# The third batch's first quad takes its memory weights through a turn in DRAM in place of five TensorE transposes, with two instruction orders drawn up again

## The chip, the cores and the metric

One NeuronCore of a Trainium2 chip runs the whole program. The metric is the device time of one execution in microseconds (us), the median of several runs.

## The reference, cut to what matters

Eight batches, eight heads, 576 rows (`S`), head width 64, 32 memory slots (`M`); `d_model` is 512.

```python
a = softmax(phi, over the 576 rows)           # phi: batch, head, 576, 32
k_m = einsum('bhsm,bhsd->bhmd', a, k)         # keys and values of the 32 slots
v_m = einsum('bhsm,bhsd->bhmd', a, v)
attn = softmax(q @ k_m.T / 8)                 # 576 x 32 for each head
x = attn @ v_m                                # heads side by side: 576 x 512
u = x + (relu(x.T @ w_tok1) @ w_tok2).T       # mixing over rows, 256 wide
out = u + relu(u @ w_ch1) @ w_ch2             # mixing over channels, 1536 wide
```

## The kernel before

**Quads.** Four heads of a batch form a quad; there are sixteen, named here (batch, half). A quad's 4 x 32 slots fill the 128 partitions. For each quad the kernel takes the softmax of phi over rows (`phi_max` on DVE, `phi_exp` on ACT, `scales`/`phi_scale` on DVE), multiplies the weights with keys and values (`get_kv`, L641 or `mm_kv`, L1482: 20 matmuls into `kvp`), spreads the keys (`spread_T`), turns them (`turn_T`), copies them (`get_kb`), and forms the scores (`scores`, tiles `sp`). Their softmax goes out to DRAM and back by rows (`rows_out` L517, `rows_in` L524), is split in a high and a low part (`nat`), and the token mixing follows: `A` (tile `Ap`), `R` (`Rp`), and four products `u`, whose results are split in `uh` (ACT, L198) and `ul` (DVE, L201).

**Chunks.** The rows of all batches are cut in nine chunks of 512 columns. Chunks 0 to 2 go through the channel mixing directly: `mm_1` (L144, tile `cp`, 12 matmuls for each of 12 blocks), a relu split in `hh` and `hl`, and `ch2` (L167, tile `acc`). Chunks 3 to 8 go in three pairs through another scheme (`Pair`, `Run`, L298 and L2318), which fills the second half of the program.

**Three ways to the weights of phi.** `kvp` needs the exponentials with rows on the partitions. The quads of batches 0 and 1 (`EarlyQuad`) load phi so that the softmax runs along the free axis and then turn it by five TensorE transposes of 128x128 (`phi_turn`, L1125, tiles `pp`), which ACT copies out of PSUM (`phi_get`, L1148). The quads from (2,1) on (`LateQuad`) load another layout (`in_phi_turned_dram`, tile `phiT`), turn blocks of 32x32 on DVE (`phi_turn`, L628), write the result to DRAM (`phi_out`, two DMAs of L517, tensor `turns`) and read it back rearranged (`phi_in`, two DMAs of L524). Quad (2,0), here `second`, is of its own class `ThirdBatchQuad` and goes the first way, by transposes.

**Two orders.** The instruction order is written out, not found at run time. `step` registers a piece of work with its engine, its cost in us, what it waits for, and the rooms (buffers, PSUM banks) that it takes or uses; `plan` runs through them with a rank for each step and gives every engine its order; the steps are then issued in that order. It is done twice. The first order (numbers `RANKS`, L1043) covers the weights' conversion (`piece`), quads (0,0) to (1,1), chunk 0, and for (2,0) the loads and its turning of phi. The second (numbers `PLACES`, L2110) covers the other quads, from `get_kv` of (2,0) on, and chunks 1 and 2. The steps' costs stand beside them: `scores` 1.0 us, `get_kv` 1.25 us. In the first order `ps_tile` puts in matmuls of the identity with itself (L1075, `z.fill` of them) where the plan leaves TensorE a gap ahead of a step that takes a bank.

Each engine works through its own queue in order, SP's queue of DMA issues too. TensorE writes PSUM banks of three kinds (`at`, two; `acc0` to `acc3`; `ch`, two). The transposes of (2,0) take two `at` banks; its `kvp` takes a `ch` bank.

```python
            s.x_t = z = step(
                "PE", 0.65, lambda: s.phi_turn([b0, b1]), z, take=[b0, b1], use=[s.phi]
            )
...
    second = ThirdBatchQuad(2, 0)
    second.phi, kv2, q2 = Room(("phi", 2)), Room(("kv", 1)), Room(("qT", 1))
    second.l_phi = step("SP", 0.5, second.load_phi, take=[second.phi], move=0.9)
    z = second.plan_phi()
```

Of the kernel before, what the change touches and what calls it, by code (L numbers as in the profile page):

```python
# [10 lines left out]
F32 = mybir.dt.float32  # L11
# [9 lines left out]
P = 128  # L21
# [7 lines left out]
def kernel(  # L29
# [936 lines left out]
    def plan(rank, ways, slack=0.0, margin=0.85, behind=1e9):  # L966
# [644 lines left out]
    class ThirdBatchQuad(SecondQuad):  # L1611

        for name in (
            "turn_T", "get_kb", "scores", "S_take", "turn_S", "rows_in", "nat_low", "a_high", "a_low",
            "v_pair", "A", "R", "u", "straight", "u_high", "u_low", "spill", "store_u",
        ):
            locals()[name] = vars(LateQuad)[name]

        def spread_v(s, room):
            LateQuad.vb_room(s, room)  # L1620
            s.spread_values(s.vb, s.kvp[:, D : 2 * D])

        def get_kv(s):
            s.kvp = pch.tile([P, CW], F32, tag="ch", name="kvp" + s.n, bufs=2)
            s.mm_kv()

# [135 lines left out]
    second = ThirdBatchQuad(2, 0)  # L1762
    second.phi, kv2, q2 = Room(("phi", 2)), Room(("kv", 1)), Room(("qT", 1))
    second.l_phi = step("SP", 0.5, second.load_phi, take=[second.phi], move=0.9)
    z = second.plan_phi()
# [3 lines left out]
    for x in range(NKK):  # L1769
# [5 lines left out]
        "END", 0, None, z, second.scaled, took2, products[-1], *ready[NF - 1][:2],  # L1775
        *(y for Q in range(2) for y in quads[1, Q].lows + quads[1, Q].highs),
        use=[*PartC2.held, *room1, rest_room, second.phi, second.ptr, second.colr, kv2, q2, o0, *accs, *ready[NF - 1][2:], *room0],
# [15 lines left out]
    ahead = [(quads[1, 0].x_u[3].end, late[1].load_turned)] + [(118.0, late[1].phi_max)]  # L1793
# [11 lines left out]
    def room(tag, n=1):  # L1805
        return Room((tag, n))
# [7 lines left out]
    kv2, q2, pt2 = room("kv"), room("qT"), room("aT")  # L1814
# [3 lines left out]
        take=[*sum(c1_rooms, []), *u_rooms[1], o_rooms[0], rest_room, *hidden[0, NF - 1], kv2, q2, pt2, turned1, col1],  # L1818
# [46 lines left out]
    for n, qd in enumerate(late):  # L1865
        t0, do = later(n)
        if not n:
            qd.kvuse, qd.after, qd.q_r, qd.lq = [pt2, kv2], [begin], q2, begin
            continue
# [7 lines left out]
        z = do(-38, "ACT", 0.8, qd.phi_exp, y, use=[turned, col])  # L1877
# [10 lines left out]
    got_kv = do(-9, "PE", 1.25, second.get_kv, begin, take=[bank_rooms[0]], use=second.kvuse)  # L1888
    for n, qd in enumerate(late):
        t0, do = later(n)  # L1890
        bk, kb, vh, vl, vb = bank_rooms[n], kb_rooms[n], vh_rooms[n], vl_rooms[n], Room(("side vb", 1), ("vb", 1))
        T = room("kb") if n else room("pr", 2)
        z = got_kv
        if n:
            y = do(-8, "ACT", 0.37, qd.spread_T, z, qd.scaled, take=[T], use=[bk, qd.colr])
        else:
            y = do(-8, "DVE", 0.35, qd.spread_T, z, take=[T], use=[bk])
        v = do(-8, "DVE", 0.48, lambda qd=qd, r=vb: qd.spread_v(r), z, qd.scaled if n else y, sided, take=[vb], use=[bk, side_room] + [qd.colr] * (n > 0))
# [8 lines left out]
        z = do(0, "PE", 1.0, qd.scores, y, qd.lq, take=[*ss, S_], use=[qd.q_r, kb])  # L1907
        if nx:
            got_kv = do(0.1, "PE", 1.25, nx.get_kv, z, *nx.after, *vlows[-1:], take=[bank_rooms[n + 1]], use=nx.kvuse)
# [196 lines left out]
    for n in range(AHEAD):  # L2106
# [424 lines left out]
```

## Time and profile before

| what | value |
|---|---|
| median of 3 runs (lowest, highest) | 716.09 us (715.88, 717.05) |
| the profiled execution's own time | 718.54 us |
| its span, first to last instruction | 716.8 us |
| TensorE busy | 706.3 us, 99% |
| VectorE (DVE), ScalarE (ACT), GpSimd (POOL) busy | 521.9, 372.2, 60.2 us |
| bytes moved by DMA, mean rate | 157.08 MB, 219 GB/s |

The profiled execution is 2.45 us above the median; 1.74 us of it lie outside the span. In the rows further down `PEld` is TensorE's weight load, which runs beside its matmuls; a start is counted from the span's first instruction; what stands in square brackets is the idle time ahead of a row and what ended it. An f32 matmul is recorded as two, so a step of 20 shows as x40.

### The profile page before, as it was taken

How to read it: one execution, taken by the hardware profiler on the slowest of the kernel's cores; microseconds unless marked ns; L12 is line 12 of the kernel's file. 1: busy time of each engine (PE TensorE's matmuls, PEld its weight loads, DVE VectorE, ACT ScalarE, POOL GpSimd, SP SyncE). 2: the span in 40 equal slices, each digit the busy share in tenths (PEclk: the TensorE clock that was granted, in tenths of full speed). 3: DMA queues.
4: the chain of work that ended last, by engine and by line, in shares of the span. 5: the costliest groups of instructions: out<-in, count | busy, mean ns of one | idle time of the engine just before them, and what ended most of it. 6: DMA issues, size and time to landing. Idle time of an engine off the chain costs nothing.

```text
span 716.8 us, 11389 instructions
## 1 busy us (share of the span) xinstructions
PE 706.3 (99%) x4305; PEld 587.8 (82%) x4305; DVE 521.9 (73%) x861; ACT 372.2 (52%) x697; POOL 60.2 (8%) x64
## 2 busy tenths in 40 slices
PE   8899999999999999999999999999999999999998
PEld 8678888778888788889888888888888888788887
DVE  5999973877878986788665669976238976426983
ACT  6899774335455266546554465425346444436450
POOL 2133114010012201011100000000000000000000
PEclk9999999999999999999999999999999999999999
DMA  9966440878979999836627875284658074658202
GB/s 357 415 252 253 122 154 18 309 252 283 302 272 300 325 374 320 273 113 212 214 90 268 293 273 197 85 282 132 206 196 303 31 262 149 201 181 292 91 29 89
DMA packets 75334, 157.08 MB, mean 219 GB/s; under 512 B 16144, under 2 KB 38416, under 8 KB 70928
## 3 DMA queue, kind: packets, MB, share of 16 engines
q1 hardware_dynamic: 61600, 102.29, 40.4%
q10 hardware_dynamic: 13680, 54.07, 23.0%
q8 instruction: 34, 0.56, 0.3%
q14 instruction: 20, 0.16, 0.1%
HBM read 115.93 MB, written 40.40 MB: 218 GB/s over the span
## 4 chain that ended last, share of the span: by engine, by line
PE 86%; DMA 7%; DVE 5%; issue 1%; ACT 1%; SPq 0%; DVEq 0%; ACTq 0%
PE ma L298 13%; PE acc L167 12%; PE cp L144 12%; PE mU L2318 10%; PE mB L2318 7%; PE mc L298 7%; PE u L748 6%; PE mD L2318 3%; PE mA L2318 3%; PE mb L298 3%; PE Ap L551 3%; DMA phiT<-in_phi_turned_dram 2%; DMA raww<-in_w_tok_dram 2%; PE kvp L641 1%; DMA unit<-sums 1%; PE u L567 1%
## 5 line engine op out<-in xcount | busy, mean ns | idle before, releaser
L167 PE MATMUL acc<-hh,c 128*128 128x512 f32 x288 | 101.5, 399 | 0.0
L167 PEld LDWEIGHTS acc<-hh,c 128*128 128x128 f32 x288 | 54.1, 188 | 13.6 <-issue 2.6
L167 PE MATMUL acc<-hl,c 128*128 128x512 f32 x144 | 56.3, 391 | 0.0
L144 PE MATMUL cp<-uh,c1h 128*128 128x512 f32 x144 | 52.0, 402 | 0.4 <-DVE col L623 0.4
L144 PE MATMUL cp<-ul,c1h 128*128 128x512 f32 x144 | 50.5, 391 | 0.0
L144 PE MATMUL cp<-uh,c1l 128*128 128x512 f32 x144 | 50.4, 390 | 0.0
L2304 ACT CAST rT<-hid 128x512 fp32r<-128x512 f32 x54 | 32.1, 623 | 26.7 <-PE mB L2318 15.6
L2305 DVE TENSOR_TENSOR rT<-hid,rT 128x512 fp32r<-128x512 f32 x54 | 35.8, 686 | 6.7 <-ACT rT L2304 6.7
L691 POOL TENSOR_TENSOR nat<-side,nat 128x512 fp32r<-128x512 f32 (+1 forms) x24 | 22.8, 951 | 179.9 <-ACT nat L682 134.6
L2172 DVE TENSOR_TENSOR hid<-mb,hid 128x512 f32<-128x512 f32 x12 | 8.3, 692 | 39.0 <-ACT hid L2252 37.8
L114 ACT ACTIVATE hh<-cp 128x512 fp32r<-128x512 f32 x36 | 21.6, 599 | 24.4 <-PE cp L144 22.0
L117 DVE SCALAR_TENSOR_TENSOR hl<-cp,hh 128x512 fp32r<-128x512 f32 x36 | 24.6, 683 | 12.9 <-ACT hh L114 12.7
L144 PEld LDWEIGHTS cp<-uh,c1h 128*128 128x128 f32 x144 | 26.7, 188 | 8.7 <-issue 3.4
L2175 ACT ACTIVATE hid<-hid 128x512 f32<-128x512 f32 x24 | 15.2, 634 | 34.7 <-DVE hid L2172 34.7
L758 ACT COPY side<-u 128x288 f32<-128x288 f32 (+1 forms) x44 | 17.1, 392 | 28.9 <-PE u L748 26.8
L144 PEld LDWEIGHTS cp<-uh,c1l 128*128 128x128 f32 x144 | 27.0, 188 | 5.9
L144 PEld LDWEIGHTS cp<-ul,c1h 128*128 128x128 f32 x144 | 27.1, 188 | 4.6
L2304 ACT CAST r<-hid 128x512 fp32r<-128x512 f32 x36 | 22.5, 625 | 15.8 <-PE mU L2318 5.3
L167 PEld LDWEIGHTS acc<-hl,c 128*128 128x128 f32 x144 | 27.1, 188 | 4.1
L2305 DVE TENSOR_TENSOR r<-hid,r 128x512 fp32r<-128x512 f32 x36 | 24.7, 687 | 5.4 <-ACT r L2304 5.4
L298 PE MATMUL ma<-xrest_p,unit 128*128 128x512 f32 x108 | 27.4, 389 | 0.0
L748 PE MATMUL u<-w2h,Rh 128*128 128x288 f32 x96 | 27.0, 296 | 0.0
(380 smaller groups left out, 1900.9 us busy)
## 6 DMA issues: line engine op xcount, KB each, us to landing
unit<-sums ACTq DMA_DIRECT2D x54, 512.0 KB, 5.0
kv<-in_kv_dram ACTq DMA_DIRECT2D x11, 1280.0 KB, 8.3
rawc<-in_w_ch_dram SPq DMA_DIRECT2D x12, 1024.0 KB, 9.1
q<-in_q_dram ACTq DMA_DIRECT2D x11, 576.0 KB, 5.4
sums<-sums SPq DMA_DIRECT2D x12, 512.0 KB, 5.5
u_p<-spilled SPq DMA_DIRECT2D x6, 1024.0 KB, 6.6
unit<-sums ACTq DMA_DIRECT2D x18, 256.0 KB, 3.9
out_dram<-u_p SPq DMA_DIRECT2D x9, 512.0 KB, 2.8
```

Source lines behind the costliest of these rows:

```text
L114: nc.scalar.activation(out=h, in_=ps, func=AF.Relu)
L117: nc.vector.scalar_tensor_tensor(out=l, in0=ps, scalar=0.0, in1=f32(h), op0=ALU.max, op1=ALU.subtract)
L144: nc.tensor.matmul(ps, l[:, a], r[:, a], start=n == 0, stop=n == len(mm) - 1)
L167: nc.tensor.matmul(ps, l_[f // 2][:, f % 2, a * P : (a + 1) * P], r[:, w], start=f == start and x == 0, stop=f == end - 1 and x == 2,)
L298: nc.tensor.matmul(ps, l, r, start=first and n == 0, stop=n == len(mm) - 1, skip_group_check=not first,)
L551: nc.tensor.matmul(ps[:, :TT], a, w, start=x == 0, stop=x == len(mm) - 1)
L691: eng.tensor_tensor(out=o, in0=a, in1=f32(h), op=ALU.subtract)
L748: nc.tensor.matmul(s.up[db, hf][:, :HALF], a, r, start=x == 0, stop=x == len(mm) - 1)
L758: nc.scalar.copy(out=side[0][:, o + n : o + HALF], in_=ps[:, n:HALF])
L2304: nc.scalar.copy(out=t[:, 0], in_=x)
L2305: nc.vector.tensor_tensor(out=t[:, 1], in0=x, in1=f32(t[:, 0]), op=ALU.subtract)
L2318: nc.tensor.matmul(s.banks[room][a][:, w], l_[:, a * P : a * P + P], r_, start=not (p or x) and name in ("11", "T1", "21", "T4"), stop=p = ...
```

## The change

Quad (2,0) becomes a `LateQuad`. Its phi is loaded turned, its blocks are turned on DVE, written to DRAM and read back rearranged, within the first order; the five transposes, their two ACT copies and the class `ThirdBatchQuad` go. Its keys are spread on ACT in place of DVE. In the second order the cost of `scores` is 0.65 us (1.0 before), that of `get_kv` 1.36 us (1.25), that of `phi_exp` 0.88 us (0.8). Both tables of numbers are new, and with them the place of every step.

```diff
     RANKS = (
-        782, 764, 736, 674, 772, 710, 644, 470, 574, 316, 176, 288, 108, 64, 136, 122, 774, 216, 54,
+        784, 754, 704, 660, 774, 692, 568, 280, 448, 688, 182, 524, 160, 416, 86, 246, 778, 358,
...
-    class ThirdBatchQuad(SecondQuad):
...
-    second = ThirdBatchQuad(2, 0)
-    second.phi, kv2, q2 = Room(("phi", 2)), Room(("kv", 1)), Room(("qT", 1))
-    second.l_phi = step("SP", 0.5, second.load_phi, take=[second.phi], move=0.9)
-    z = second.plan_phi()
+    second = LateQuad(2, 0)
+    turned2, col2, phi2, kv2, q2 = (Room(x) for x in (("al", 2), ("ps", 2), ("phi", 2), ("kv", 1), ("qT", 1)))
+    z = step("SP", 0.5, second.load_turned, take=[turned2], move=0.81)
+    z = step("DVE", 0.78, second.phi_max, z, take=[col2], use=[turned2])
+    z = step("ACT", 1.0, second.phi_exp, z, use=[turned2, col2])
+    scaled = step("DVE", 0.38, second.scales, z, use=[col2])
+    turn2 = z = step("DVE", 0.8, second.phi_turn, z, take=[phi2], use=[turned2])
+    z = step("SP", 0.9, second.phi_out, z, use=[phi2], move=0.81)
+    z.lands = True
+    z = step("SP", 0.9, second.phi_in, z, use=[phi2], move=1.18)
...
-    ahead = [(quads[1, 0].x_u[3].end, late[1].load_turned)] + [(118.0, late[1].phi_max)]
+    ahead = [(turn2.end, late[1].load_turned), (max(turn2.end + 4.0, 118.0), late[1].phi_max)]
...
-        z = do(-38, "ACT", 0.8, qd.phi_exp, y, use=[turned, col])
+        z = do(-38, "ACT", 0.88, qd.phi_exp, y, use=[turned, col])
...
-    got_kv = do(-9, "PE", 1.25, second.get_kv, begin, take=[bank_rooms[0]], use=second.kvuse)
+    got_kv = do(-9, "PE", 1.36, second.get_kv, begin, take=[bank_rooms[0]], use=second.kvuse)
...
-        T = room("kb") if n else room("pr", 2)
+        T = room("kb")
         z = got_kv
-        if n:
-            y = do(-8, "ACT", 0.37, qd.spread_T, z, qd.scaled, take=[T], use=[bk, qd.colr])
-        else:
-            y = do(-8, "DVE", 0.35, qd.spread_T, z, take=[T], use=[bk])
...
+        y = do(-8, "ACT", 0.37, qd.spread_T, z, qd.scaled, take=[T], use=[bk, qd.colr])
...
-        z = do(0, "PE", 1.0, qd.scores, y, qd.lq, take=[*ss, S_], use=[qd.q_r, kb])
+        z = do(0, "PE", 0.65, qd.scores, y, qd.lq, take=[*ss, S_], use=[qd.q_r, kb])
...
-    order = plan(dict(zip(steps, PLACES, strict=True)), dict.fromkeys(steps, 0), 0.3969, 3.3, 5.0043)
+    order = plan(dict(zip(steps, PLACES, strict=True)), dict.fromkeys(steps, 0), 0.3837, 3.1511, 4.9562)
```

The diff leaves one thing unsaid that the counts of the orders show: over the program TensorE issues 5 transposes fewer and 9 identity matmuls more; DVE gets the turn of (2,0), one pass of a magnitude from ACT, and the low parts of a weight piece and of an attention operand from POOL, and gives one spreading of keys to ACT.

**TensorE at the end of the first order**, where quad (1,1) ends (`u11_1_1`), (2,0) begins and chunk 1 follows. Before:

```order
L567 MATMUL u11_1_1_1348<-w2l_97,Rh_1_1_1289 128x288
L567 MATMUL u11_1_1_1348<-w2h_96,Rl_1_1_1291 128x288
L1125 MATMUL pp0_2_0_1362<-ident_74,phi_2_0_163 128x128 x4
L1125 MATMUL pp1_2_0_1363<-ident_74,phi_2_0_163 128x128
L1482 MATMUL kvp_2_0_1379<-kv_2_0_799,pt_2_0_1369 32x128 x20
L144 MATMUL cp0_1_1409<-uh_1_864,c1h0_486 128x512
```

And now:

```order
L567 MATMUL u11_1_1_1365<-w2l_97,Rh_1_1_1287 128x288
L567 MATMUL u11_1_1_1365<-w2h_96,Rl_1_1_1290 128x288
L641 MATMUL kvp_2_0_1386<-kv_2_0_756,phi_2_0_561 32x128 x20
L144 MATMUL cp0_1_1415<-uh_1_847,c1h0_512 128x512
L144 MATMUL cp0_1_1415<-ul_1_848,c1h0_512 128x512
```

The two rows of transposes are gone, and the keys and values follow the last `u`.

**SP's queue in the first 20 us** (`raww2` is w_tok2, `rawc1_0` the first blocks of w_ch1, `rawc1_4` later ones). Before:

```order
L1093 DMA q_0_1_127<-in_q_dram 128x1152
L876 DMA raww2_1_131<-in_w_tok2_dram 128x1152
L876 DMA raww2_0_134<-in_w_tok2_dram 128x1152
L1255 DMA v_0_1_136<-in_kv_dram 128x1280
L896 DMA rawc1_0_158<-in_w_ch1_dram 128x2048
L896 DMA rawc1_4_160<-in_w_ch1_dram 128x2048
L1097 DMA phi_2_0_163<-in_phi_dram 128x640
L922 DMA rawc2_0_167<-in_w_ch2_dram 128x2048
L1097 DMA phi_1_0_219<-in_phi_dram 128x640
```

And now:

```order
L610 DMA phiT_2_0_127<-in_phi_turned_dram 128x576
L1093 DMA q_0_1_131<-in_q_dram 128x1152
L876 DMA raww2_1_134<-in_w_tok2_dram 128x1152
L876 DMA raww2_0_136<-in_w_tok2_dram 128x1152
L1255 DMA v_0_1_158<-in_kv_dram 128x1280
L896 DMA rawc1_4_160<-in_w_ch1_dram 128x2048
L1097 DMA phi_1_0_163<-in_phi_dram 128x640
L896 DMA rawc1_0_167<-in_w_ch1_dram 128x2048
L922 DMA rawc2_0_172<-in_w_ch2_dram 128x2048
```

The turned phi of (2,0) stands ahead of q, both pieces of w_tok2 and v; the first piece of w_ch1 has moved behind `rawc1_4` and the phi of (1,0).

**TensorE where chunk 0 begins** (`Tp` is the keys' transpose of (1,0), `cp0_0` the first product of chunk 0). Before:

```order
L1482 MATMUL kvp_1_0_556<-kv_1_0_299,pt_1_0_549 32x128 x20
L144 MATMUL cp0_0_586<-uh_0_474,c1h0_486 128x512 x4
L144 MATMUL cp0_0_586<-ul_0_475,c1h0_486 128x512 x4
L144 MATMUL cp0_0_586<-uh_0_474,c1l0_487 128x512 x4
L1500 MATMUL Tp_1_0_607<-ident_74,T_1_0_582 128x128
L144 MATMUL cp1_0_609<-uh_0_474,c1h0_486 128x512 x4
```

And now:

```order
L1482 MATMUL kvp_1_0_565<-kv_1_0_302,pt_1_0_540 32x128 x20
L1075 MATMUL Tp_1_0_603<-ident_74 128x128 x2
L1500 MATMUL Tp_1_0_603<-ident_74,T_1_0_597 128x128
L1075 MATMUL sp0_1_0_618<-ident_74 128x128 x2
L463 MATMUL sp0_1_0_618<-q_1_0_269,kb_1_0_612 32x288
L463 MATMUL sp1_1_0_621<-q_1_0_269,kb_1_0_612 32x288
```

Before, the first product of chunk 0 stood between the keys and values of (1,0) and their transpose, and the scores came after the second product; now transpose and scores (six more rows of `sp`) come ahead of the first product, with two identity matmuls in front of each.

## Rows read from the trace of the kernel before

**Rows 1.** The page's first part: busy time, share of the span, instructions.
```profile
PE 706.3 (99%) x4305; PEld 587.8 (82%) x4305; DVE 521.9 (73%) x861; ACT 372.2 (52%) x697; POOL 60.2 (8%) x64
```
**Rows 2.** Stretches: length, busy of each engine (x instructions), PEclk, DMA share, GB/s.
```profile
0.00:41.86 41.86, 37.34 (x416) 31.73 (x416) 31.78 (x58) 32.63 (x59) 9.39 (x22) 1.00 0.96 385
41.86:123.00 81.14, 80.84 (x463) 67.02 (x459) 66.26 (x94) 60.78 (x96) 22.30 (x14) 1.00 0.43 144
...
126.00:320.00 194.00, 192.79 (x1563) 158.06 (x1563) 155.86 (x290) 93.24 (x220) 24.18 (x24) 1.00 0.86 287
```
**Rows 3.** TensorE's waits: line, releaser, us in total, times, longest.
```profile
PE Rp L1075 <- ACT A L1374: 1.0, 1, 1.0
...
PE Ap L551 <- DVE ul L201: 0.5, 1, 0.5
PE cp L144 <- DVE col L623: 0.4, 1, 0.4
```
**Rows 4.** Timeline of TensorE, end of the first order: start, us, instruction.
```profile
122.88 0.29 PE L567 MATMUL u<-w2h,Rl 128*128 128x288 f32 x1
123.09 0.66 PE L1125 MATMUL pp<-ident,phi 128*128 128x128 f32 x4
124.08 0.33 PE L1125 MATMUL pp<-ident,phi 128*128 128x128 f32 x1 [0.33 <-DVE ul L201]
124.48 1.30 PE L1482 MATMUL kvp<-kv,pt 128*32 128x128 f32 x40
125.70 0.50 PE L144 MATMUL cp<-uh,c1h 128*128 128x512 f32 x1
```
**Rows 5.** Timeline of DVE at the same place.
```profile
123.69 0.33 DVE L201 TENSOR_TENSOR ul<-u,uh 128x160 fp32r<-128x160 f32 x1 [0.66 <-ACT uh L198]
```
**Rows 6.** Timeline of TensorE up to chunk 0.
```profile
30.85 0.71 PE L1075 MATMUL Rp<-ident 128*128 128x128 f32 x4 [1.01 <-ACT A L1374]
31.40 1.03 PE L1378 MATMUL Rp<-vb,A 128*128 128x256 f32 x4
...
35.54 1.24 PE L1406 MATMUL u<-aT,vb 64*128 64x288 f32 x8
...
40.63 1.30 PE L1482 MATMUL kvp<-kv,pt 128*32 128x128 f32 x40
41.86 1.18 PE L144 MATMUL cp<-uh,c1h 128*128 128x512 f32 x4
...
48.62 0.71 PE L463 MATMUL sp<-q,kb 64*32 64x288 f32 x14 [0.30 <-DVE vb L1134]
49.27 0.50 PE L167 MATMUL acc<-hh,c 128*128 128x512 f32 x1
```
**Rows 7.** The chain that ended last: start us, us; an early load, a product of chunk 0.
```profile
7.49 12.21 DMA raww<-in_w_tok_dram
...
52.29 2.72 PE cp L144 x12
```
**Rows 8.** Timeline of ACT: the first piece of w_ch1 is there.
```profile
23.79 1.27 ACT L805 ACTIVATE rawc<-rawc,mask 128x1024 f32<-128x1024 uint32 x1 [0.18 <-DMA rawc<-in_w_ch_dram]
```
**Rows 9.** Timeline of TensorE: keys and values by way of DRAM, quad (2,1).
```profile
147.34 1.43 PE L641 MATMUL kvp<-kv,phi 64*32 64x128 f32 x40
148.70 0.50 PE L167 MATMUL acc<-hh,c 128*128 128x512 f32 x1
```
**Rows 10.** DMA issues from 110 to 320 us: count, size, median us to landing.
```profile
turns<-phi SPq DMA_DIRECT2D x11, 256.0 KB, 6.6
phi<-turns SPq DMA_DIRECT2D x11, 256.0 KB, 5.0
```
**Rows 11.** Timeline of SP's queue.
```profile
41.99 0.80 SPq L1476 DMA_DIRECT2D kv<-in_kv_dram  x2
```
**Rows 12.** Timeline of DVE: a magnitude pass, the turn of a quad's phi.
```profile
29.37 0.70 DVE L823 TENSOR_SCALAR rawc<-rawc 128x1024 int32<-128x1024 int32 x1
...
125.77 0.76 DVE L628 STREAM_TRANSPOSE phi<-phiT 128x576 f32<-128x576 f32 x1
```

More of the change, by code (lines that the diff above doesn't have):

```diff
@@ L1609, in plan @@
             return s.highs[0]
-    class ThirdBatchQuad(SecondQuad):
[L1613 to L1625, printed above, removed]
     converted = []
@@ L1774 @@
     step(
-        "END", 0, None, z, second.scaled, took2, products[-1], *ready[NF - 1][:2],
+        "END", 0, None, z, scaled, took2, products[-1], *ready[NF - 1][:2],
         *(y for Q in range(2) for y in quads[1, Q].lows + quads[1, Q].highs),
-        use=[*PartC2.held, *room1, rest_room, second.phi, second.ptr, second.colr, kv2, q2, o0, *accs, *ready[NF - 1][2:], *room0],
+        use=[*PartC2.held, *room1, rest_room, phi2, col2, kv2, q2, o0, *accs, *ready[NF - 1][2:], *room0],
     )
@@ L1813 @@
     hidden = {(0, NF - 1): (room("hh", 2), room("hl", 2))}
-    kv2, q2, pt2 = room("kv"), room("qT"), room("aT")
+    kv2, q2, phi2, col2 = room("kv"), room("qT"), room("phi", 2), room("ps", 3)
     turned1, col1 = room("al", 2), room("ps", 3)
@@ L1817 @@
         "END", 0, None,
-        take=[*sum(c1_rooms, []), *u_rooms[1], o_rooms[0], rest_room, *hidden[0, NF - 1], kv2, q2, pt2, turned1, col1],
+        take=[*sum(c1_rooms, []), *u_rooms[1], o_rooms[0], rest_room, *hidden[0, NF - 1], kv2, q2, phi2, col2, turned1, col1],
     )
@@ L1867 @@
         if not n:
-            qd.kvuse, qd.after, qd.q_r, qd.lq = [pt2, kv2], [begin], q2, begin
+            qd.kvuse, qd.after, qd.q_r, qd.lq = [phi2, kv2], [begin], q2, begin
+            qd.scaled, qd.colr = begin, col2
             continue
@@ L1891 @@
         bk, kb, vh, vl, vb = bank_rooms[n], kb_rooms[n], vh_rooms[n], vl_rooms[n], Room(("side vb", 1), ("vb", 1))
-        T = room("kb") if n else room("pr", 2)
+        T = room("kb")
         z = got_kv
-        if n:
-            y = do(-8, "ACT", 0.37, qd.spread_T, z, qd.scaled, take=[T], use=[bk, qd.colr])
-        else:
-            y = do(-8, "DVE", 0.35, qd.spread_T, z, take=[T], use=[bk])
-        v = do(-8, "DVE", 0.48, lambda qd=qd, r=vb: qd.spread_v(r), z, qd.scaled if n else y, sided, take=[vb], use=[bk, side_room] + [qd.colr] * (n > 0))
+        y = do(-8, "ACT", 0.37, qd.spread_T, z, qd.scaled, take=[T], use=[bk, qd.colr])
+        v = do(-8, "DVE", 0.48, lambda qd=qd, r=vb: qd.spread_v(r), z, qd.scaled, sided, take=[vb], use=[bk, side_room, qd.colr])
         y = do(-7, "PE", 0.12, qd.turn_T, y, v, use=[bk, T])
@@ L1906 @@
         nx = late[n + 1] if n + 1 < len(late) else None
-        z = do(0, "PE", 1.0, qd.scores, y, qd.lq, take=[*ss, S_], use=[qd.q_r, kb])
+        z = do(0, "PE", 0.65, qd.scores, y, qd.lq, take=[*ss, S_], use=[qd.q_r, kb])
         if nx:
-            got_kv = do(0.1, "PE", 1.25, nx.get_kv, z, *nx.after, *vlows[-1:], take=[bank_rooms[n + 1]], use=nx.kvuse)
+            got_kv = do(0.1, "PE", 1.36, nx.get_kv, z, *nx.after, *vlows[-1:], take=[bank_rooms[n + 1]], use=nx.kvuse)
         z.not_before = t0
@@ L2490, in _lay @@
         kv=np.stack([rows(k, 0), rows(v, 0)], axis=3).transpose(0, 1, 2, 3, 5, 4, 6),
-        phi=turned.reshape(rows_phi.shape)[:3],
+        phi=turned.reshape(rows_phi.shape)[:2],
         phi_turned=whole[2:],
```

134 rows, old and new, of tables (PLACES, RANKS) are left out of this document.

## The prediction

> **What bounds the kernel now.** I read the page's first part, then busy time by stretch, TensorE's waits, its timeline at the two places that the change touches, and the chain of waits. TensorE is busy for 706.3 of the 716.8 us of the span; the next engine, DVE, for 521.9 [rows 1]. So a step off TensorE, or a wait of TensorE less, shows in the end one for one, and work on another engine only if TensorE comes to wait for it. By stretches the idle time of TensorE is 41.86 - 37.34 = 4.52 us before chunk 0 begins, 0.30 us from there to 123, and 1.21 us from 126 to 320, where the second order ends [rows 2]. What comes after 320 us the change does not touch. The granted clock is 1.00 (2.4 GHz) in all of them, so prices are taken at that clock.
>
> Two places matter. At 123 us the transposes of (2,0) stand between the last `u` of (1,1) and chunk 1 [rows 4]. In the first 42 us TensorE waits for a chain that begins with loads: the DMA engines are busy for 0.96 of that time at 385 GB/s [rows 2], the chain that ended last sits for 12.21 us, to 19.70, on w_tok2 [rows 7], and TensorE's longest wait there is one of 1.01 us for ACT [rows 3, 6].
>
> **The change, part by part.**
>
> *The transposes go.* The last `u` is issued at 122.88; `u` of 288 columns follow one another every 0.13 us, so TensorE is free for the next at 123.01. `kvp` starts at 124.48: 1.47 us for five transposes [rows 4]. Part of it is waiting: the fifth one took 0.33 us of idle time until DVE had read the bank of an earlier `u` [rows 4, 5]. `kvp` itself needs a bank of another kind, so nothing of this is left for it; I keep 0.05 us for the step from one form to the other. Removed: 1.42 us.
>
> *`kvp` in its new form.* Before it takes 125.70 - 124.48 = 1.22 us [rows 4]; with weights that came through DRAM, on (2,1), 148.70 - 147.34 = 1.36 us [rows 9]. Added: 0.14 us. **This place: 1.28 us less.** Bounds: 0.8 us, if a wait of 0.5 us like the one of `Ap` in rows 3 shows up behind it, since the spreading of keys now stands in ACT's queue and that of values behind the turn of (2,1) on DVE; 1.47 us at most.
>
> A rule speaks against the exchange. The Trainium skill, "VectorE: DVE Perf Modes", section "Rules for kernel authors", sends a 128x128 transpose to TensorE whenever a PSUM destination will do. By it the five would stay and this term would be 0; the rows have TensorE as the bound and the other way's engines with room at 123 us, and I go by the rows.
>
> *The way through DRAM.* Two writes and two reads per quad, 6.6 and 5.0 us to landing [rows 10], some 12 us in all, and a turn on DVE of 0.76 us [rows 12]. All of it now happens between 40 and 55 us, some 70 us before `kvp` of (2,0) wants it: nothing on the path. SP's queue: the two writes stand ahead of the load of k and v for (1,1), which before was issued at 41.99 [rows 11], once `kvp` of (1,0) had ended and freed its buffer (at 41.86 [rows 6]); the turn is done by then too. The two reads wait for the writes, issued near 41.5 and landed near 48.1, and the load of `rawc1_6` stands behind them. Cost 0; if that cover fails, a load is late by a us or two in a stretch where the DMA engines are busy for 0.43 of the time [rows 2].
>
> *The load moved ahead.* The turned phi, 128 x 576 x 4 bytes = 0.295 MB, is moved ahead of q, w_tok2 and v in SP's queue. At 385 GB/s [rows 2] it puts them off by 0.77 us, on the very chain that the head waits for [rows 7]. So I start quad (0,1)'s `A` 0.8 us later.
>
> *The head's new order.* From there I follow TensorE. Before, quad (0,1)'s `R` waits 1.01 us and is padded by 0.55 us of identity matmuls (two, from 30.85 to 31.40) [rows 6]. Now half of quad (0,0)'s `u` (12 of 0.13 us) stands in that place and covers the wait; 1.56 us less. Against it stand the 0.8 us of the load and the transposes of (1,0), which now come ahead of the `u` of (0,1) with two identity matmuls (0.6 us, most of it the 0.66 of four such transposes in rows 4, and 0.55). So the first matmul of that `u` comes at some 35.9 by this sum (35.54 before); I take 35.6, since (0,0)'s second half no longer waits behind ACT's eviction of `A`, and its end and `kvp` of (1,0), no longer broken by those transposes, come 0.6 us earlier in relation to it: `kvp` ends at 41.3 in place of 41.86 [rows 6].
>
> Then the new order loses. Before, from 41.86 to 49.27, TensorE did two products of chunk 0 (2.72 us each [rows 7], 5.45 us), the keys' transpose and the scores, with a wait of 0.30 us: 1.96 us besides the products [rows 6]. Now transpose and scores come first, and each waits for its predecessor on DVE or ACT with only identity matmuls beside it. I put 0.2 us more for each of the three hand-overs, an estimate from the 0.30 us that one of them cost before: 2.5 us in all. 41.3 + 2.5 + 5.45 = 49.25 against 49.27. **The head: 0**, between 1.5 less (the 1.01 us of waiting gone for good, and no dearer hand-overs) and 2.5 more (the second rival).
>
> *The new costs of `scores` and `get_kv`* only shift places. The second order lists the same work; its stretch had 1.21 us of idle time [rows 2], of which the largest pieces are 0.5 us ahead of an `Ap` and 0.4 us ahead of a `cp` [rows 3]. I cannot read from the order which of them come back; I take 0, with 1.2 us less and as much more as bounds.
>
> **The sum.** 1.28 + 0 + 0 = 1.3 us less: 718.54 - 1.3 = 717.2 for the profiled execution. That one stands 2.45 us above the median, so the median goes from 716.09 to **714.8**.
>
> **The rivals.**
>
> *Both orders close their gaps (712.9).* If the second order sheds its 1.2 us of idle time, and the head's hand-overs cost 0.7 us less than I put: 714.8 - 1.9. For it: the planner now has the durations that the trace shows. Against it: such waits come from banks and queues, not from these two costs.
>
> *The head gives the gain back (716.1).* The first piece of w_ch1 now comes behind `rawc1_4` and phi of (1,0): 1.05 + 0.33 MB, 3.6 us at 385 GB/s, and 0.77 us for the turned phi. Before it was there at 23.79 and its first product began at 41.86, 18.1 us later [rows 6, 8]. Landing at 28.1, with the same 18.1 us, that product would begin at 46.2 in place of 43.8 (41.3 + 2.5): 2.4 us more, 717.2. Its conversion then had much queueing in it, which the new order cuts, so half of it is likelier: 1.2 to 1.3 us, 716.1.
>
> *DVE sets the head's end (718.5, slower).* DVE gets in the first order the turn (0.76), a magnitude pass (0.70), and the low parts of a weight piece and an attention operand, which I price like these two (0.70 and 0.76): 2.9 us [rows 12]. It is busy for 31.78 of the first 41.86 us and 66.26 of the next 81.14 [rows 2]. If the conversions of w_ch1 run as one chain behind the loads, then 2.9 + 0.77 us come to the end and the 1.42 us of transposes less 0.14 go off it: 716.09 + 3.67 - 1.28 = 718.5. It decides once DVE's slack ahead of chunk 0's third product, when the second piece of w_ch1 is wanted, is under that. Against it: before, TensorE idles only 0.30 us between 42 and 123 although DVE is near full [rows 2].
>
> That the change does not do what it says is ruled out by the order: the transposes are gone from their place.
>
> **How the numbers follow.** Forecast 714.8: 0.42. Gaps closed 712.9: 0.25. Head gives it back 716.1: 0.18. DVE 718.5: 0.15. About 0.2%, 1.43 us, can be told from no change here; faster by more is below 714.66, just under the forecast, which takes somewhat less than half of its chance: 0.19 + 0.25 = 0.44. Within 0.2%: 0.23 + 0.18 = 0.41. Slower: 0.15. The bounds of the terms, 0.8 to 1.47 us at the transposes, 1.5 less in the head and 1.2 less or more in the second order, and the case of 717.2 reach from 712.1 to 717.3 if they are never all met at once; to leave no more than 2 in 10 out, some 1 on each side, I take **712.6 to 717.6**.
>
> **What would show it.** Right: at some 122 us `kvp` follows `u` with no idle time, its start some 1.4 us earlier; `acc` of chunk 0 still begins near 49.2; TensorE idles about 1.2 us between 124 and 318. Wrong by the second rival: the first `cp` of chunk 0 begins after 44.5 behind a wait for `c1h` or `c1l`. Wrong by the third: waits of TensorE for DVE between 44 and 75, with DVE without a gap. Wrong by the first: idle time of the second order well under 1. A wait of keys' transpose or scores of (2,0) that takes the place of the five transposes would make the first term wrong.

## The result

The change made the kernel slower. Its median is 720.64 us against 716.31 us for the kernel before (six executions each); the ratio is 1.0051, 95% interval 1.0035 to 1.0067, so about 3.7 us. The forecast was 714.8 us, and 720.6 lies above the range's end of 717.6. (One execution of the changed kernel, of some 3.4 ms, is left out of the ratio; without it the median would be 720.40.)

The profiled execution of the changed kernel took 720.40 us, with a span of 718.5 us. That is only 1.9 us over the profiled one of before, which lay 2.2 us above that kernel's median of 716.31. So this pair of profiles shows about half of the loss; a second profile of the changed kernel, further below, shows more of it.

The page's first part for the changed kernel (busy time, share of the span, instructions):

```profile
PE 707.7 (98%) x4318; PEld 590.2 (82%) x4318; DVE 526.0 (73%) x864; ACT 369.5 (51%) x695; POOL 56.3 (8%) x62
```

TensorE is busy 1.4 us longer than in [rows 1], although five transposes are gone: nine identity matmuls came in. The same stretches as in [rows 2] (length, busy time of each engine, granted clock, DMA share, GB/s):

```profile
0.00:41.86 41.86, 39.04 (x413) 33.43 (x417) 32.10 (x56) 31.35 (x55) 9.30 (x22) 1.00 0.97 389
41.86:123.00 81.14, 79.17 (x469) 65.74 (x461) 69.18 (x99) 60.09 (x97) 16.96 (x12) 1.00 0.44 149
126.00:320.00 194.00, 191.36 (x1580) 157.81 (x1578) 148.21 (x275) 93.16 (x221) 23.73 (x22) 1.00 0.85 286
```

Idle time of TensorE is 2.82 us in the first stretch (4.52 before), 81.14 - 79.17 = 1.97 us in the second (0.30 before) and 2.64 us in the third (1.21 before). TensorE's waits (line, releaser, us, times, longest) put most of the second and of the third down to one wait each:

```profile
PE Rp L729 <- ACT Ah L717: 2.5, 1, 2.5
PE Tp L1500 <- DVE T L1129: 1.6, 1, 1.6
```

**The head.** TensorE's timeline (start, us, instruction, idle time before it and its releaser) where chunk 0 should begin; before, a `cp` stood right behind this `kvp` [rows 6]:

```profile
41.10 1.30 PE L1482 MATMUL kvp<-kv,pt 128*32 128x128 f32 x40
42.33 0.71 PE L1075 MATMUL Tp<-ident 128*128 128x128 f32 x4
44.65 0.33 PE L1500 MATMUL Tp<-ident,T 128*128 128x128 f32 x1 [1.61 <-DVE T L1129]
45.33 0.71 PE L1075 MATMUL sp<-ident 128*128 128x128 f32 x4 [0.36 <-ACT kb L1504]
45.97 0.72 PE L463 MATMUL sp<-q,kb 64*32 64x288 f32 x16
46.62 1.20 PE L144 MATMUL cp<-uh,c1h 128*128 128x512 f32 x4
...
52.67 0.47 PE L167 MATMUL acc<-hh,c 128*128 128x512 f32 x1
```

`kvp` ends at 42.33, 1.0 us after the forecast, and the first `cp` comes 4.29 us later, where I had put 2.5. The 1.0 us are there before this place: the `u` of (0,1) begins at 36.56, where I took 35.6, and its `A` (tile `Ap`) at 27.44. TensorE's timeline further ahead:

```profile
26.38 0.61 PE L1075 MATMUL Ap<-ident 128*128 128x128 f32 x4
27.44 2.73 PE L1368 MATMUL Ap<-raww,k 128*128 128x256 f32 x10 [0.45 <-DVE k L1336]
...
36.56 1.24 PE L1406 MATMUL u<-aT,vb 64*128 64x288 f32 x8
```

From `kvp` on it is the hand-overs. The keys' `T` (L1129), which DVE spreads, is what TensorE waits for longest. VectorE's timeline up to it:

```profile
38.02 3.49 DVE L811 SCALAR_TENSOR_TENSOR rawc<-rawc 128x1024 int32<-128x1024 int32 x1
41.44 1.21 DVE L828 SCALAR_TENSOR_TENSOR rawc<-rawc 128x1024 f32<-128x1024 f32 x1
42.57 0.74 DVE L201 TENSOR_TENSOR ul<-u,uh 128x288 fp32r<-128x288 f32 x2
43.23 0.76 DVE L628 STREAM_TRANSPOSE phi<-phiT 128x576 f32<-128x576 f32 x1
43.92 0.41 DVE L201 TENSOR_TENSOR ul<-u,uh 128x288 fp32r<-128x288 f32 x1
44.27 0.33 DVE L1129 TENSOR_SCALAR T<-kvp,col 128x128 f32<-128x128 f32 x1
```

VectorE has no gap, the turn of (2,0) stands ahead of `T`, and the L811 at 38.02 takes 3.49 us, where this form takes 1.22 when it runs alone (low_on_vector, below). L811 is the pass that joins the two halves of a weight's bits; both of its inputs are in SBUF, as are those of POOL's low part (L839). (The recorded expectations call it a magnitude; that is L823.) POOL's timeline shows what ran beside it:

```profile
37.64 2.79 POOL L839 TENSOR_TENSOR c1l<-rawc,c1h 128x1024 fp32r<-128x1024 f32 x1 [8.96 <-ACT c1h L835]
```

POOL's low part ends at 40.43; L811 ends 1.08 us after that, as if it had begun only then. The Trainium skill, "SBUF — State Buffer", section "SBUF: two separate sides", says that a VectorE instruction with two SBUF inputs and a GpSimd instruction that reads SBUF share a pair of ports as an exclusive lock, which the one that starts first holds for its whole instruction. By that rule L811 would end at 40.43 + 1.2 = 41.6; the trace says 41.51 and agrees to some 0.1 us.

**The end of the first order.** TensorE's timeline; [rows 4] answer to it:

```profile
125.88 1.43 PE L641 MATMUL kvp<-kv,phi 64*32 64x128 f32 x40
127.25 0.50 PE L144 MATMUL cp<-uh,c1h 128*128 128x512 f32 x1
```

No idle time is marked ahead of `kvp`, as the forecast had it. But chunk 1 starts at 127.25, 1.55 us later than before.

**The second order.** The wait of 2.50 us for `Ah`, quad (2,0)'s rounded `A`. ACT's timeline:

```profile
162.85 0.60 ACT L114 ACTIVATE hh<-cp 128x512 fp32r<-128x512 f32 x1 [0.43 <-PE cp L144]
169.85 0.34 ACTq L606 DMA_DIRECT2D q<-in_q_dram  x1
170.29 0.68 ACT L485 ACTIVATE S<-S 128x576 f32<-128x576 f32 x1 [6.84 <-DMA turns<-phi]
170.88 0.35 ACT L717 CAST Ah<-Ap 128x256 fp32r<-128x256 f32 x1
```

ACT stands still for 6.4 us ahead of the issue of one load of q (that of quad (3,1)); the exponential of another quad and `Ah` queue behind it, with their data there (TensorE's last `Ap` matmul ends at 167.4). The bracket names `turns<-phi`, a DMA, as what ended that time. SP's queue and the DMA issues from 155 to 175 us (count, KB, us to landing) show what the load waited for:

```profile
162.14 0.32 SPq L517 DMA_DIRECT2D turns<-phi  x1
```

```profile
turns<-phi SPq DMA_DIRECT2D x1, 256.0 KB, 7.6
```

162.14 + 7.6 = 169.74, and the load goes out at 169.85. It reads nothing that this DMA writes. What ties the two is a counter: the program gives its counters to its DMAs in turn, and a DMA waits until the one that had its counter before has landed. The rows of the program, with what each waits for, show the same counter for both (the first is the way out of the phi of (4,0), in SP's queue, the second the load in ACT's):

```
L517 DMA turns_4_0_1791<-phi_0_1775 128x512 [waits DMAHW1_49,DVE_49]
L606 DMA q_1_1817<-in_q_dram 128x1152 [waits DMAHW1_49,PE_49]
```

From 320 us on the trace names no wait of TensorE in the changed kernel, so the 0.7 us that before waited for a load of `unit` at 624 came back.

### The profile page after: what moved, and what is told of

Its sections match the earlier page's. It is cut to its first block, busy times and chain, and to the rows that moved or that the text cites. A ratio compares the mean times of both kernels' runs of the same rounds, so it can differ in the third digit from the quotient of the medians.

```text
span 718.5 us, 11432 instructions
## 1 busy us (share of the span) xinstructions
PE 707.7 (98%) x4318; PEld 590.2 (82%) x4318; DVE 526.0 (73%) x864; ACT 369.5 (51%) x695; POOL 56.3 (8%) x62
## 4 chain that ended last, share of the span: by engine, by line
PE 91%; DMA 4%; DVE 3%; issue 1%; ACT 0%; SPq 0%; ACTq 0%; DVEq 0%
PE ma L298 14%; PE cp L144 13%; PE acc L167 13%; PE mU L2306 10%; PE u L748 7%; PE mB L2306 7%; PE mc L298 7%; PE mD L2306 3%; PE mb L298 3%; PE mA L2306 3%; PE Ap L551 3%; PE kvp L641 2%; DMA raww<-in_w_tok_dram 2%; PE Rp L729 1%; PE u L567 1%
## 5 line engine op out<-in xcount | busy, mean ns | idle before, releaser
L2293 DVE TENSOR_TENSOR rT<-hid,rT 128x512 fp32r<-128x512 f32 x54 | 35.9, 690 | 6.0 <-ACT rT L2292 6.0
```

The lines of the kernel that those rows point to most:

```text
L2293: nc.vector.tensor_tensor(out=t[:, 1], in0=x, in1=f32(t[:, 0]), op=ALU.subtract)
```

## The experiments

"Before" was timed again beside the runs, in four groups; its medians were 716.6 to 716.8 us, and each ratio is to the before of its own group. Starts are those of the profiled execution.

| run | median us | ratio to before (95%) | first `cp` | chunk 1 |
|---|---|---|---|---|
| before | 716.3 | | 41.86 | 125.70 |
| changed | 720.64 | 1.0051 (1.0035 to 1.0067) | 46.62 | 127.25 |
| changed_again | 720.93 | 1.0064 (1.0046 to 1.0083) | 47.20 | 128.80 |
| dram_only | 715.82 | 0.9985 (0.9977 to 0.9993) | 41.97 | 124.62 |
| second_new | 716.56 | 1.0004 (0.9992 to 1.0016) | 42.19 | 123.84 |
| first_new | 720.78 | 1.0059 (1.0031 to 1.0086) | 47.05 | 128.65 |
| filled_gap | 720.55 | 1.0055 (1.0039 to 1.0072) | 46.65 | 127.32 |
| low_on_vector | 719.45 | 1.0042 (1.0026 to 1.0058) | 44.65 | 125.28 |
| turn_late | 721.51 | 1.0065 (1.0051 to 1.0080) | 47.41 | 128.48 |
| second_q_late | 714.65 | 0.9970 (0.9959 to 0.9982) | 41.98 | 123.63 |
| q_late | 719.87 | 1.0038 (1.0025 to 1.0051) | 46.47 | 128.69 |
| q_late_low | 716.59 | 0.9997 (0.9988 to 1.0005) | 45.58 | 126.20 |
| load_ahead | 715.67 | 0.9980 (0.9971 to 0.9989) | 42.94 | 124.58 |
| transposes_back | 716.13 | 0.9989 (0.9980 to 0.9998) | 42.19 | 125.08 |
| q_late_filled | 717.90 | 1.0015 (1.0006 to 1.0024) | 47.89 | 128.53 |

### The replacement and the two orders apart

`RANKED` and `PLACED` are the orders of before, written out step for step, with buffers and identity matmuls. **dram_only** uses both, **second_new** only `RANKED`, **first_new** only `PLACED`. In all three ACT spreads the keys of (2,0), as in the change.

```diff
-    order = plan({z: x // 2 for z, x in zip(steps, RANKS, strict=True)}, {z: x % 2 for z, x in zip(steps, RANKS)}, margin=1.05)
+    order = written(steps, RANKED)
...
-    order = plan(dict(zip(steps, PLACES, strict=True)), dict.fromkeys(steps, 0), 0.3837, 3.1511, 4.9562)
+    order = written(steps, PLACED)
```

> Both orders of before, written out step for step; of the change only the way through DRAM: phi of (2, 0) is loaded turned where phi was loaded, its transpose on DVE and the two DMAs stand right behind its scale step at about 65 us, the five transposes and their two copies are gone. Theory A (the replacement is worth its 1.3 us, the two new orders lost it): 1.3 us under before, about 715.0, with kvp of (2, 0) right behind u and chunk 1 starting near 124.3. Rival B (the way through DRAM itself costs: its load at the head, its turn on VectorE, its traffic): not below before, 716.3 or more, with chunk 1 not before 125.7.

1.0 us below before in the medians, 1.1 by the ratio, a little less than the 1.3 expected: Theory A holds, B falls. TensorE's timeline of dram_only at the end of the first order:

```profile
123.04 0.29 PE L567 MATMUL u<-w2h,Rl 128*128 128x288 f32 x1
123.26 1.43 PE L641 MATMUL kvp<-kv,phi 64*32 64x128 f32 x40
124.62 0.50 PE L144 MATMUL cp<-uh,c1h 128*128 128x512 f32 x1
```

From the last `u` to chunk 1 it is 1.58 us, against 125.70 - 122.88 = 2.82 in [rows 4]: 1.24 us less, where the forecast had 1.28.

> As the run with both old orders, but with the new second order and its costs. Theory A: the new second order holds a wait of 2.5 us of TensorE at Rp L729 behind the load of q on ACT, against 1.2 us of idle time in the old one, so 1 to 2.5 us above the run with both old orders: 716 to 717.5. Rival C (the whole loss is the second order's): 719 or more. Rival D (the whole loss is the head's): as the run with both old orders, 715.

0.7 us above dram_only by the medians, 1.4 by the ratios. The wait at `Rp` is there (2.8 us, below), yet less of it shows. C falls; against D the two intervals only just overlap.

> The changed kernel with its new first order, but with the second order of before written out (the new spread of the keys on ACT stays). Theory A: chunk 1 starts at 127.2 as in the changed kernel (TensorE waits 1.6 us for VectorE at T of (1, 0) near 43), 1.5 us later than in before, and no new wait in the second order: 717.5 to 718.3. Rival C (the loss is the second order's): 715 to 716. Rival D (the loss is the head's): 720.

720.78 us, 5 above dram_only. It is the first order that loses; C falls, and D, that the head has the whole loss, is nearer than A. But the written second order does not fit the other beginning: TensorE's waits of first_new between 126 and 320 us show a new one of 2.2 us, so this run is no clean measure of the first order alone.

```profile
PE kvp L658 <- DVE side L1134: 2.2, 1, 2.2
```

> The changed kernel once more, for a second profile on the chip of the other three. Theory A: 720.5, with both waits again, 1.6 us for VectorE near 43 and 2.5 us for ACT near 169. If one of the two waits is absent in this profile, it is not what makes the median.

Both waits are back (1.62 and 2.1 us), and this profile shows one thing more. TensorE's busy time and granted clock by the microsecond (then DMA share, GB/s):

```profile
43.00:44.00 1.00, 0.05 (x1) 1.00 0.10 39
44.00:45.00 1.00, 0.33 (x1) 1.00 0.12 45
45.00:46.00 1.00, 0.65 (x4) 0.94 0.75 250
46.00:47.00 1.00, 1.00 (x17) 0.50 1.02 118
...
48.00:49.00 1.00, 1.00 (x3) 0.50 0.94 364
49.00:50.00 1.00, 1.00 (x5) 0.86 1.03 423
```

After the gap TensorE is granted half its clock, 1.2 in place of 2.4 GHz, for some 3.4 us, and chunk 0's products run through it: chunk 1 starts at 128.80, 1.55 us later than in the first profile, which had 1.00 throughout. Over the executions of the two timings the mean granted clock is 0.998 or less in six of eleven, and these took 1.5 to 2 us more than the others (720.9 against 719.4 in the first timing, 722.0 against 720.0 in the second). That is what the one pair of profiles could not show.

### What makes T late

**filled_gap**: nine identity matmuls, not two, ahead of the keys' transpose.

```diff
+    quads[1, 0].x_T.fill = 9
     late = [second] + [LateQuad(2, 1)] + [LateQuad(b, Q) for b in range(3, B) for Q in range(2)]
```

> The changed kernel with nine in place of two matmuls of the identity ahead of the transpose of T of (1, 0), so that TensorE works while it waits for VectorE between 43 and 44.6; T comes no sooner. Theory A (the late T costs twice: some 2 us of waiting, and in most executions some 1.7 us more since TensorE is granted half its clock for about 3.5 us after the gap): the granted clock stays 1.00 from 45 to 50, chunk 1 starts at 127.2 as before, and the median falls by 1 to 1.7 us, to 719 to 720, with a narrower spread. Rival E (the half clock has another cause, or is nothing but the slow runs): median and spread as in the changed kernel, 720.5 to 721.

Median unchanged, as Rival E had it; three of six executions are still at 0.998. The profiled one held 1.00, with 2.0 us of waiting still at `Rp`, so where the others lost the clock it does not show. This was left for q_late_filled.

**low_on_vector**: POOL's c1l goes to VectorE.

```diff
+    h, l = w_c[0][0]
+    l.eng = "DVE"
+    order.remove(l)
+    order.insert(max(order.index(converted[5].done), order.index(h) + 1), l)
```

> The changed kernel with one low part of chunk 0 (c1l, 2.8 us on POOL at 37.6) on VectorE, in front of the L828 at 41.4. Theory A (the magnitude L811 on VectorE took 3.49 in place of 1.2 us because POOL's low part ran beside it, and T of (1, 0) stood behind it): L811 takes 1.2 us, T is done some 0.8 us sooner (43.8 in place of 44.6) although VectorE has 1.2 us more to do, and the wait at Tp falls from 1.6 to about 0.8; 1 to 2 us below the changed kernel, 719 to 720. Rival F (VectorE simply has too much to do there, L811 waits for its data): L811 stays long or T comes 1.2 us later, 721.5 or more.

VectorE's timeline of this run:

```profile
37.19 1.22 DVE L811 SCALAR_TENSOR_TENSOR rawc<-rawc 128x1024 int32<-128x1024 int32 x1
38.33 1.22 DVE L839 TENSOR_TENSOR c1l<-rawc,c1h 128x1024 fp32r<-128x1024 f32 x1
...
42.30 0.33 DVE L1129 TENSOR_SCALAR T<-kvp,col 128x128 f32<-128x128 f32 x1
```

L811 is back at 1.22 us. With one instruction more, VectorE is earlier at `T` by 1.97 us (part of it because all of this profile's head runs some 0.5 us earlier: `kvp` starts at 40.59, not 41.10). The wait at `Tp` is gone; F falls. The median falls by 1.2 us only: the wait at `Rp` is still there (2.3 us), and three of eight executions are at 0.998 or less.

**turn_late**: the turn of (2,0) and the maximum of (1,1)'s phi move behind the last low part of `u` of chunk 0, and the write of the turn to DRAM with them.

```diff
+    last = max(order.index(z) for z in a.lows + c.lows)
+    for z in (turn2, quads[1, 1].scaled.after[0].after[0]):
+        if order.index(z) < last:
+            order.remove(z)
+            order.insert(last, z)
...
```

> The changed kernel with VectorE's turn of phi of (2, 0) (0.76 us) and the maximum of phi of (1, 1) (0.80) moved behind the last low part of u of chunk 0. Theory A: T is done 0.76 us sooner, the wait at Tp falls to 0.9, and the gap is shorter; 1 to 1.5 us below the changed kernel, 719.4 to 720. Rival D (the order around does it, not VectorE's load): no change, 720.5 or more.

A miss: no gain. VectorE's timeline of this run says why; once the turn was out of the way, a low part waited for ACT, and `T` came only 0.25 us sooner. The L811 still takes 3.48 us.

```profile
38.01 3.48 DVE L811 SCALAR_TENSOR_TENSOR rawc<-rawc 128x1024 int32<-128x1024 int32 x1
...
43.64 0.46 DVE L201 TENSOR_TENSOR ul<-u,uh 128x288 fp32r<-128x288 f32 x1 [0.36 <-ACT uh L198]
44.02 0.34 DVE L1129 TENSOR_SCALAR T<-kvp,col 128x128 f32<-128x128 f32 x1
```

So the turn is not what makes `T` late; by low_on_vector, the collision is.

### The load of q

**second_q_late** is second_new with one step moved:

```diff
...
+    order.remove(late[3].lq)
+    order.insert(order.index(late[0].x_Ah) + 1, late[3].lq)
```

> The first order of before with the way through DRAM and the new second order (716.56 with a wait of 2.8 us at Rp L729), with one step moved: the load of q that stood in ACT's queue in front of the rounding Ah of (2, 0) stands behind it. Theory A (the load waits for an earlier DMA to land, and Ah stands behind it): no wait over 0.3 us at Rp L729, 1 to 2.5 us below that run: 714 to 715.5, the lowest of all so far. Rival G (Ah is late for another reason, its own data or the ACT work before it): the wait stays, 716.5.

714.65 us, the lowest of all, 2.0 us under before. ACT's timeline of this run: the load still waits, until 167.43, but `Ah` is done by then.

```profile
163.84 0.37 ACT L717 CAST Ah<-Ap 128x256 fp32r<-128x256 f32 x1
167.43 0.33 ACTq L606 DMA_DIRECT2D q<-in_q_dram  x1
```

`Rp` of (2,0) starts without a wait, where it waited 2.78 us in second_new; G falls. TensorE's timeline of second_q_late, and then of second_new:

```profile
165.02 0.40 PE L729 MATMUL Rp<-vh,Ah 128*128 128x256 f32 x2
```

```profile
168.16 0.50 PE L729 MATMUL Rp<-vh,Ah 128*128 128x256 f32 x2 [2.78 <-ACT Ah L717]
```

**q_late** makes the same move in the changed kernel:

> The changed kernel with the load of q that blocked ACT moved behind the rounding Ah of (2, 0), nothing else. Theory A (two gaps of TensorE, near 43 and near 169, each costs its own length and in part of the executions a stretch at half the granted clock): the wait at Rp L729 is gone, the one at Tp stays with 1.6 us; 1.5 to 2.5 us below the changed kernel, 718.0 to 719.0. Rival H (the gap near 43 alone makes the median): 720 or more.

719.87 us, some 1 us less and not the 1.5 to 2.5 expected, so nearer to Rival H (720 or more) than to Theory A, though the wait at `Rp` is gone. Four of five executions are at 0.998: the gap near 43 is still there, and the profile has half the clock from 46.7 to 50.1.

**q_late_filled** is q_late with filled_gap's nine identity matmuls:

> The changed kernel with the load of q behind Ah (719.87, granted clock 0.998 in four of five executions, with the half clock from 45 to 50 in the profile) and with nine matmuls of the identity in place of two ahead of the transpose of T, so that the gap near 43 is filled though T comes no sooner. Theory A (the idle gap makes the granted clock fall, and that is worth about 1.5 us beside the 2 us of waiting): granted clock 1.00 in nearly all executions and 718.0 to 718.7. Rival L (the clock falls there whatever TensorE is given to do in the gap, or falls elsewhere): 0.998 in most executions and 719.5 to 720.

717.90 us, 2.0 us less by the medians and 1.6 by the ratios, although the first `cp` comes no sooner. Ten of eleven executions are at 0.999 or 1.00. Theory A holds: the idle gap made the clock fall. The profiles agree: of the five with that gap open, the clock fell behind it in four (changed_again, first_new, turn_late, q_late; not in the first one of the changed kernel); of the four with it filled or shortened (filled_gap, low_on_vector, q_late_low, q_late_filled), in none. The eleventh is the profiled one; its clock fell elsewhere (near 20 us, after a wait of 0.9 us in the head) and not after the filled gap near 44. Two profiles with the old first order, second_new and transposes_back, fell at the same place after a wait of 1.1 us, and 5 of the 80 executions of before in the four groups are at 0.998, so this gap is not the only one that costs the clock. The profile of q_late_filled:

```profile
20.00:22.00 2.00, 2.00 (x10) 0.50 1.03 428
...
44.00:46.00 2.00, 1.97 (x18) 1.00 0.00 0
```

**q_late_low** has both repairs, the load behind `Ah` and c1l on VectorE:

> The changed kernel with both repairs: that load of q behind Ah, and the low part c1l on VectorE. Theory A: no wait of TensorE over 0.8 us is left apart from the start's, no execution at a granted clock under 1.00, chunk 1 starts at 125.3; 715.8 to 717.0, at or below before. What is left above the 714.65 us of the old first order is the first order's own. Rival I (the clock falls in these orders without a gap of TensorE): some executions at 0.998 or less stay, and the median is over 718.

716.59 us, level with before; no execution under 0.999. Chunk 1 starts at 126.20, not the 125.3 expected, with 0.48 us of waiting left at `Tp`, within the 0.8 that Theory A allowed. Rival I falls. The two repairs together give 4 us, and each by itself about 1: with either gap left, part of the executions still lose the clock.

### The prediction's other terms

**load_ahead** is second_q_late with the load where the change put it:

```diff
+    z = turn2.after[0].after[0].after[0]
+    order.remove(z)
+    order.insert(order.index(c.l_q), z)
```

> The run that was lowest so far (first order of before with the way through DRAM, new second order, load of q behind Ah: 714.65) with one step moved: the load of the turned phi of (2, 0) stands ahead of q of (0, 1), as in the changed kernel, and not behind two loads of weights. The prediction's term (0.77 us on the head's chain, since the loads there run one behind another): the first cp starts at 42.7 in place of 42.0, and the time is 715.2 to 715.5. Rival J (the load's time is hidden in the waits of the head): first cp at 42.0, 714.6.

The first `cp` comes at 42.94 in place of 41.98, and the time is 1.0 us higher by the medians, 0.7 by the two ratios: the term is real and of its size. Rival J falls. TensorE's timeline (the scores of (0,1) wait for their q, which they did not in second_q_late; then the `R` of (0,0) waits 1.58 us, 0.59 in second_q_late):

```profile
16.58 2.34 PE L1290 MATMUL sp<-kb,q 128*128 128x64 f32 x20 [0.71 <-DMA q<-in_q_dram]
26.38 1.13 PE L1378 MATMUL Rp<-vb,A 128*128 128x256 f32 x4 [1.58 <-ACT A L1374]
```

**transposes_back** is the kernel before with the new second order and the load of q behind `Ah`:

> The first order of before with its transposes of phi of (2, 0) kept, the new second order, and the load of q behind Ah: against the run at 714.65 us only the way through DRAM is taken back. The prediction's term 1: 1.3 us slower than that run, 715.9, chunk 1 at 125.7. Theory A says the same for it; and that the new second order with its one step mended is then worth some 0.6 us by itself against before. Rival K (the way through DRAM is worth nothing): 714.7.

716.13 us, 1.5 us above second_q_late (1.4 by the ratios, 1.3 expected), 0.7 under before. K falls.

## Why the prediction was wrong

**The transposes (1.28 us less): right.** 1.24 us in the traces, 1.0 and 1.5 us in the two pairs of medians. The rule of the Trainium skill that I set against it, by which this term would be 0, is not borne out in this kernel; the second wait of 0.5 us that I held possible did not come in dram_only.

**The way through DRAM (0): right for itself.** dram_only carries it whole and gains. What the prediction counted as "nothing on the path" holds with the turn behind its scale step, at 68.82 us in that trace. In the new order the turn stood in front of `T`, and even that was not the cause (turn_late).

**The load moved ahead (0.77 us): right**, 0.7 to 1.0 us.

**The head's new order (0): this is the step that failed.** In the first profile, all of it at full clock, chunk 1 starts 1.55 us later although the transposes gave back 1.24, so the head with the load ahead costs 2.8 us where I put 0 and bounded it at 2.5. Some 1.0 us of it stands ahead of `kvp`: my own sum gave 35.9 for the `u` of (0,1), I took 35.6, and it began at 36.56, with `A` of that quad 1.1 us later than before (27.44 against 26.33) and not 0.8, behind two identity matmuls and a wait of 0.45 us. The rest is the hand-overs. I wrote "I put 0.2 us more for each of the three hand-overs". The first of them, from `kvp` to `Tp`, took 2.3 us instead, because VectorE came late with `T`: one pass of L811 beside POOL's low part cost 3.49 us in place of 1.2. I had priced the moved instructions by rows in which they run alone, and had not asked what POOL does beside them, although the trace of before had shown the same collision, at another place. VectorE's timeline of before, and POOL's:

```profile
26.86 2.48 DVE L811 SCALAR_TENSOR_TENSOR rawc<-rawc 128x1024 int32<-128x1024 int32 x1
```

```profile
26.60 1.66 POOL L839 TENSOR_TENSOR w2l<-raww,w2h 128x576 fp32r<-128x576 f32 x1 [6.97 <-ACT w2h L835]
```

Again VectorE ends 1.08 us after POOL. The plan keeps such pairs apart, and had this pass of the changed kernel ahead of POOL's low part; on the chip POOL began 0.4 us sooner, and VectorE waited.

**"The granted clock is 1.00 (2.4 GHz) in all of them, so prices are taken at that clock": failed too.** A gap of TensorE of 2 us is charged twice, once as waiting, and in more than half of the executions again as some 3.4 us at half the clock. That is 2.0 us of the median, 1.6 by the ratios (q_late against q_late_filled). A term for it was in no rival.

**The second order (0, within 1.2): failed by its sign and size in the trace** (2.64 us of idle time for 1.21), by a wait that the order could have shown: a load in ACT's queue that waits for an earlier DMA, with `Ah` behind it. The prediction asked what stands behind SP's DMAs and not what stands behind ACT's. Mended, the same order is faster than the old one by 0.7 us with the transposes (transposes_back against before) and by 1.2 us with the way through DRAM (second_q_late against dram_only; 1.1 by the ratios), so from about half to all of the 1.2 us that my first rival gave it.

**The rivals.** The third, that VectorE sets the head's end, named the right engine, and its sign was right: TensorE waits for VectorE near 44, and VectorE has no gap. Its mechanism was not. It added up 2.9 us of work; low_on_vector gave VectorE 1.2 us more of it and was faster. Of the second rival's sign (the first `cp` after 44.5 behind c1h or c1l) the time was seen, 46.62, but behind `T` and the scores, not those. One reading of rows was off and entered no sum: the head's longest wait before is 1.4 us at the start, for POOL's mask, and not the 1.01 us for ACT.

**The sum as measured**, in medians: 720.6 to 720.9 for the changed kernel; about 1 us of it goes with the load of q (719.87), 2.0 with the half clock (717.90), 1.3 with the late `T` itself (716.59), 0.7 to 1.0 with the load ahead. The split goes by this order of repairs: with the wait at `Rp` left, filling the gap alone brought 0.1 to 0.4 us (filled_gap). 0.9 to 1.2 us remain to the 714.65 of second_q_late. q_late_low's TensorE still waits 0.48 and 0.36 us at the hand-overs to `Tp` and the scores, which would make up most of it; that was not tried. Also open: whether the wait at `Rp` alone makes the clock fall (no profile shows it near 169, though second_new has five of twelve executions at 0.998 or less, the profiled one by its fall near 20 us, and second_q_late none of six).

Second_q_late beats both kernels: the old first order, the way through DRAM, the new second order, and one load moved.

## What to carry to other kernels

Judge a replacement and a reordering apart: here the replacement was worth what its rows said, and the new orders that came with it cost four times as much. When instructions move, read for each one what runs beside it on an engine that it collides with elsewhere in the trace (here VectorE and POOL), and what stands behind each DMA issue in the queue of an engine that also computes. And price a new gap of TensorE as its length plus the stretch at half the clock that can follow it.

## What was not expected of the hardware

- VectorE's pass L811, with two SBUF inputs, ended 1.08 us after a low part of POOL's (L839) that had begun before it (it took 3.49, 3.48 and 2.48 us in place of 1.2); begun before POOL's it took its 1.22 us (before, at 34.69, POOL from 35.59). Low parts of `u`, one of whose inputs is in PSUM, took their usual 0.4 us beside POOL.
- A gap of TensorE of some 2 us was followed by half the granted clock for about 3.4 us in some executions and not in others of the same kernel, and in three profiles one of about 1 us near 20 us was; with the gap filled by identity matmuls, the mean clock was 0.999 or more in ten of eleven executions.
- A load on ACT's queue stood for 6.4 us behind a DMA of SP's with which it shares no data.
